# Held conversions, a reciprocal on GpSimd's queue and one store for each chunk of w_out, in a fused attention and soft-MoE kernel

## The chip, the cores and the metric

The kernel runs on one core of a Trainium2 chip. The metric is device time in microseconds of one execution, the median over repeated runs, each measured from outside the kernel. A profile is one further execution, recorded by the hardware profiler; it has its own time and its own span (from the first to the last instruction). TensorE is called PE, VectorE DVE, ScalarE ACT, GpSimd POOL and SyncE SP, as in the profile.

## The reference, cut to what matters

Three layers follow each other. `phi` is the feature map of a linear attention, the second layer has a PReLU with one slope for each hidden column, the third is a soft mixture of experts.

```python
def phi(x):                                        # q, k: 8 x 8 x 576 x 64
    proj = np.einsum('bhsd,df->bhsf', x, w_phi)    # 128 features
    proj = proj - np.max(np.abs(proj), axis=-1, keepdims=True)
    return np.concatenate([np.exp(proj), np.exp(-proj)], axis=-1)
kv  = np.einsum('bhsf,bhsd->bhfd', phi(k), v)
num = np.einsum('bhsf,bhfd->bhsd', phi(q), kv)
den = np.einsum('bhsf,bhf->bhs', phi(q), phi(k).sum(2))[..., None] + 1e-06
x   = (num / den)            # -> 4608 tokens x 512
h   = x @ w_in                                     # 512 x 2048, float64
g   = np.maximum(h, 0.0) + alpha * np.minimum(h, 0.0)
y   = g @ w_out                                    # 2048 x 512, float64
logits = y @ phi_moe                               # 32 slots
d = softmax(logits, over the tokens);  c = softmax(logits, over the slots)
slot_input = d.T @ y;  slot_out[e] = relu(slot_input[e] @ w1[e]) @ w2[e]
out = c @ slot_out
```

[...]

## The kernel before

The 4608 tokens are cut into 12 blocks of 384 and the 2048 hidden columns into 16 chunks of 128. A *slot* is one block times one chunk: 12 matmuls into the tile `ph` (`gemm`, L531 to L541, the instruction is recorded at L538), which multiply x, split into a high and a low part (`xhi`, `xlo`), by a chunk of `w_in`, split likewise. The first slot of a block uses `xhi` in its first eight matmuls and `xlo` in its last four. After a slot, ACT and DVE form the PReLU in `gT` (L545, L546). `ph` has two banks, so a slot can't start before the `gT` of the slot two earlier has been read out of its bank.

Ahead of a block stands the attention of its tokens: `q_pair` makes features of q and from them `num` and `den`; `q_finish` (L461 on) forms the reciprocal of `den` (L466, L467), spreads it over 128 partitions and multiplies `num` by it, and `scale` splits the product into `xhi` (ACT, L484) and `xlo` (DVE, L485). The spreading is done in two ways. For block 0, PE does it by matmuls into `wide` (`spread`, L488). For every other block the reciprocal goes to memory and comes back as a broadcast: two stores `rc_d<-rd` (L470), two loads `bc<-rc_d` (L475), each pair issued by SP, and the multiplication `num<-bc` (L502) waits for them. The features of K (`features`, L283: a maximum at L285, a difference at L287, two exponentials on ACT) feed the matmuls `pkv`, from which `kv` and `zt` are copied (L369, L370), one pair of heads after another; block 0 needs the first four pairs.

`conv` (L185) makes one conversion of one chunk, or of two chunks at a time: two loads into `raw`, `m = Abs` on ACT (L200), then six DVE instructions (L201, L205, L206, L207, L208, and the sum L212). The tile `m` has two buffers, `raw` three. A finished chunk of `w_in` is split into a high part (ACT, L226) and a low part (DVE, L227). A finished chunk of `w_out` is stored to `wo32` by four stores of 32 partitions each (L235), transposed on PE (L240), and multiplied by the slots' matrix (L247, L253, copy L254). A later `m` in the same buffer waits until the stores and the transposes of the earlier one have read it.

The order on each engine is made by the scheduler of the language, which goes through the work by priority and by its own estimates of times; the kernel gives every step a slot number (`at(slot, phase, ...)`, the calls from L685 on) and adds edges of order without a semaphore (`add_manual_dep(..., nosync)`) where one instruction is to stand behind another on its engine. Before, the conversions of chunks 0 to 2 of `w_in` carry such an edge to the features of K (`behind` 2, 3, 3), the others none. All DMAs are issued by SP, in the order of its queue; POOL does the maximum over partitions for the features of q (`mb<-pj`, L423) and some memsets.

Of the kernel before, what the change touches and what calls it, by code (L numbers as in the profile page):

```python
# [11 lines left out]
I32 = mybir.dt.int32  # L12
U32 = mybir.dt.uint32
AF = mybir.ActivationFunctionType
ALU = mybir.AluOpType
AX = mybir.AxisListType
# [45 lines left out]
def attention_prelu_softmoe(ctx: ExitStack, tc, qT, kT, v, wphi, w_in, w_out, alpha, phi, w1, w2, out):  # L62
    nc = tc.nc
# [8 lines left out]
    wo32 = dram.tile([NC, 128, DM], F32, name="wo32")  # L72
    gT_d = dram.tile([NDEF, NC, 128, BT], F32, name="gT_d")
    rc_d = [dram.tile([2, 32, 2, HB], F32, name=f"rc_d{i}") for i in range(2)]
# [13 lines left out]
    nosync = mybir.DependencyInfo(mybir.DependencyClass.NoSync, mybir.DependencyReason.DATA)  # L88
# [94 lines left out]
    done_k = {}  # L183

    def conv(slot, srcs, uses, behind=None):  # L185
        st = {}
        n = len(srcs)

        def load():
            st["raw"] = prep.tile([128, 2, 1024], I32, tag="raw", name="raw", bufs=3)[:, 0:n]  # L190
            for j in range(n):
                nc.sync.dma_start(st["raw"][:, j], srcs[j])

        def first():
            pair = st["raw"].rearrange("p c (n t) -> p c n t", t=2)
            st["low"], high = pair[:, :, :, 0].bitcast(U32), pair[:, :, :, 1]
            m = st["m"] = prep.tile([128, 2, 512], F32, tag="m", name="m", bufs=2)[:, 0:n]
            rest = st["rest"] = high.bitcast(F32)
            mu, ru = m.bitcast(U32), rest.bitcast(U32)
            heads = [nc.scalar.activation(m, high.bitcast(F32), AF.Abs)]  # L200
            heads.append(nc.vector.tensor_scalar(out=m, in0=m, scalar1=F64_LEAST, scalar2=F64_MOST, op0=ALU.max, op1=ALU.min))  # L201
            if behind is not None:
                for ins, other in zip(heads, done_k[behind]):
                    tc.add_manual_dep(ins.ins, other.name, nosync, reason="behind the features of K")
            nc.vector.tensor_scalar(out=mu, in0=mu, scalar1=3, scalar2=0x3FFFFFFF, op0=ALU.logical_shift_left, op1=ALU.bitwise_and)  # L205
            nc.vector.scalar_tensor_tensor(out=mu, in0=high.bitcast(U32), scalar=0xC0000000, in1=mu, op0=ALU.bitwise_and, op1=ALU.bitwise_or)  # L206
            nc.vector.tensor_scalar(out=ru, in0=mu, scalar1=0xFF800000, scalar2=None, op0=ALU.bitwise_and)  # L207
            nc.vector.scalar_tensor_tensor(out=rest, in0=st["low"], scalar=2.0 ** -52, in1=rest, op0=ALU.mult, op1=ALU.mult)  # L208

        def second():  # L210
            m = st["m"]
            mark[slot + 1] = nc.vector.tensor_tensor(out=m, in0=m, in1=st["rest"], op=ALU.add).ins  # L212
            for j, use in enumerate(uses):
                use(slot + j, m[:, j])

        at(slot - 2, "pre", load)
        at(slot, "pre", first)
        at(slot + 1, "pre", second)
# [12 lines left out]
    def use_w_out(c):  # L231
        def use(slot, w):
            st = {}
            for i in range(4):
                nc.sync.dma_start(wo32[4 * i + c // 4, 32 * (c % 4):32 * (c % 4) + 32, :], w[32 * i:32 * i + 32])  # L235

            def trans():
                pt = bank("pwt")
                for k in range(KD):
                    nc.tensor.transpose(pt[:, 128 * k:128 * k + 128], w[:, 128 * k:128 * k + 128], ident)  # L240
                st["wT"] = prep.tile([128, 512], F32, tag="wT", name="wT")
                nc.scalar.copy(st["wT"], pt)

            def product():
                pw = bank("pw", ps_l)
                for k in range(KD):
                    nc.tensor.matmul(pw[32 * k:32 * k + 32, 0:128], phi_sb[:, k, :], st["wT"][:, 128 * k:128 * k + 128], start=True, stop=True)  # L247
                st["sw"] = prep.tile([128, 128], F32, tag="sw", name="sw")
                nc.scalar.copy(st["sw"], pw[:, 0:128])

            def gather():
                pw = bank("pw2", ps_l)
                nc.tensor.matmul(pw[:, 0:32], st["sw"], tident[:, 0:32], start=True, stop=True)  # L253
                nc.vector.tensor_copy(wpr[:, c, :], pw[:, 0:32])  # L254

            at(slot + 2, "pe", trans)
            at(slot + 3, "pe", product)
            at(slot + 4, "pe", gather)
        return use
# [3 lines left out]
    def k_pair(slot, i):  # L263
        b, p = divmod(i, NP)
# [17 lines left out]

        def features(src, dst, nt, read):  # L283
            mx = att.tile([128, 4], F32, tag="mx", name="mx", bufs=4)
            nc.vector.tensor_reduce(out=mx[:, 0:nt], in_=src, axis=AX.X, op=ALU.max, apply_absolute_value=True)  # L285
            neg = dst[:, :, 1, :]
            ins = nc.vector.tensor_tensor(out=neg, in0=src, in1=mx[:, 0:nt].unsqueeze(2).to_broadcast([128, nt, F]), op=ALU.subtract).ins  # L287
            if read is not None:
                read.append(ins)
            nc.scalar.activation(dst[:, :, 0, :], neg, AF.Exp)  # L290
            done_k[i] = nc.scalar.activation(neg, neg, AF.Exp, scale=-1.0).ins, ins
# [95 lines left out]
    xhi_t, xlo_t, q_st = {}, {}, {}  # L387
# [73 lines left out]
    def q_finish(slot, n):  # L461
        st = q_st[n]

        def recip():
            rd = sm.tile([128, BT], F32, tag="dT", name="rd")[:, 0:HB]
            nc.vector.tensor_scalar(out=rd, in0=st["den"][:, 0:HB], scalar1=1e-6, scalar2=None, op0=ALU.add)  # L466
            nc.vector.reciprocal(out=rd, in_=rd)  # L467
            st["rd"] = rd
            for j in range(2 if n else 0):
                nc.sync.dma_start(rc_d[n % 2][j].rearrange("p h t -> h p t"), rd[64 * j:64 * j + 64])  # L470

        def widen():
            bc = st["bc"] = xp.tile([128, NP, BT], F32, tag="bc", name="bc")
            for j in range(2):
                nc.sync.dma_start(  # L475
                    bc[64 * j:64 * j + 64], rc_d[n % 2][j, 0:NP].rearrange("p h t -> p (h t)").unsqueeze(0).to_broadcast([64, NP, BT]))

        def scale(p):
            def go():
                if p == 0:  # L480
                    xhi_t[n] = xp.tile([128, KD, BT], F32R, tag="xhi", name="xhi")
                    xlo_t[n] = xp.tile([128, KD, BT], F32R, tag="xlo", name="xlo")
                xs = st["num"][:, p, :]
                nc.scalar.copy(xhi_t[n][:, p, :], xs)  # L484
                nc.vector.tensor_tensor(out=xlo_t[n][:, p, :], in0=xs, in1=xhi_t[n][:, p, :], op=ALU.subtract)  # L485
            return go

        def spread(p):  # L488
            wide = bank("wide", ps_h)
            together([  # L490
                lambda j=j, h=h, sl=slice(64 * j, 64 * j + 64): nc.tensor.matmul(
                    wide[sl, HB * h:HB * h + HB], ident[sl, 64 * j + 32 * h + p:64 * j + 32 * h + p + 1].to_broadcast([64, 64]), st["rd"][sl],
                    start=True, stop=True)
                for h in range(2) for j in (1, 0)])
            nc.vector.tensor_tensor(out=st["num"][:, p, :], in0=wide[:, 0:BT], in1=st["num"][:, p, :], op=ALU.mult)

        def divide(p):
            def go():
                if n == 0:
                    return spread(p)  # L500
                xs = st["num"][:, p, :]
                ins = nc.vector.tensor_tensor(out=xs, in0=st["bc"][:, p, :], in1=xs, op=ALU.mult).ins  # L502
                tc.add_manual_dep(ins, mark[max(k for k in mark if k <= slot + wait)].name, nosync, reason="behind the load")
            return go

        wait = (1, 3)[n] if n < 2 else 6
        at(slot, "post", recip)
        if n:
            at(slot + 1, "pre", widen)
        for p in range(NP):  # L510
            at(slot + wait, "post", divide(p))
        for p in range(NP):
            at(slot + wait, "post", scale(p))
# [175 lines left out]
    for n in range(NB):  # L689
# [3 lines left out]
            else:  # L693
                q_pair(NC * (n - 1) + 3 * p - 6 - (p > 0) if n > 2 else 12 + 2 * p if n > 1 else (0, 2, 5, 8)[p], n, p)
        q_finish((-22, 12)[n] if n < 2 else NC * (n - 1) + 7, n)
    for c, slot, behind in ((0, -30, 2), (1, -26, 3), (2, -22, 3), (3, -3, None)):
        conv(slot, [w_in[c].bitcast(I32)], [use_w_in], behind)
    for c in range(4, NC, 2):
        conv(c - 4, [w_in[d].bitcast(I32) for d in (c, c + 1)], [use_w_in] * 2)
    for c in range(0, NC, 2):  # L700
        conv(int(10 + 1.2 * c), [w_out[d].bitcast(I32) for d in (c, c + 1)], [use_w_out(d) for d in (c, c + 1)])
    for n in range(NDEF, NB):
# [66 lines left out]
    for step in range(-45, nslots + 4):  # L769
        slot = real.get(step)  # L770
        for fn in sched.get((step, "pre"), ()):
            fn()
        h = None
# [215 lines left out]
```

## Time and profile before

| | |
|---|---|
| runs | median 977.13 us of 3 (976.02 to 977.84) |
| the profiled execution | 975.91 us |
| its span | 973.9 us, mean granted PE clock 0.987 |
| busy: PE, DVE, ACT, POOL | 931.4 (96%), 709.7 (73%), 410.3 (42%), 148.4 (15%) us |
| chain that ended last | PE 79%, DVE 13%, ACT 4%, DMA 2% |

The profiled execution is 2.0 us longer than its span, and 1.2 us shorter than the median. The table says that PE is the bound on average. An average over 974 us hides where PE is not: the trace has to be cut into stretches for that. The granted clock is a factor on PE's speed (1.00 is 2.4 GHz, 0.50 is 1.2 GHz). In rows of the timeline the first number is the start in us from the start of the span, the second the time of the group in us, then engine, line, operation, output<-inputs by tile names, and in brackets the idle time of the engine just before and what ended it.

### The profile page before, as it was taken

What the parts mean: (1) busy time and instruction counts of PE and PEld (TensorE: products, weight loads), DVE (VectorE), ACT (ScalarE), POOL (GpSimd) and SP (SyncE); (2) the same over time, 40 slices, a digit from 0 to 9 for tenths busy, and PEclk for the clock granted to TensorE, in tenths of its full rate; (3) what the DMA queues carried; (4) which work ended last, traced back from release to release, by engine and by line L of the source; (5) the groups of instructions that cost most, each with busy time, mean ns of one, the idle gap of its engine ahead of it and who ended that gap; (6) DMA issues with size and microseconds to landing.
All of it is one profiled execution on the core that took longest, in us unless ns stands there. A gap on an engine that the chain in (4) does not pass through costs nothing.

```text
span 973.9 us, 19896 instructions
## 1 busy us (share of the span) xinstructions
PE 931.4 (96%) x8210; PEld 653.7 (67%) x8210; DVE 709.7 (73%) x1341; ACT 410.3 (42%) x789; POOL 148.4 (15%) x84
## 2 busy tenths in 40 slices
PE   7978996999999999999999999999999999899997
PEld 4546774677767676676677676776777767787444
DVE  6899996897577587767777677777766767865233
ACT  6655654545445334345345336354343351221113
POOL 5111220301201212122021122111021220000000
PEclk9979998999999999999999999999999999999999
DMA  7346665553131131021121121210111508588999
GB/s 262 116 162 206 204 207 154 176 173 114 54 87 34 31 84 44 23 78 44 35 71 42 33 72 31 70 31 23 46 34 51 178 29 269 172 270 265 329 351 327
DMA packets 75382, 121.34 MB, mean 125 GB/s; under 512 B 7836, under 2 KB 49308, under 8 KB 75292
## 3 DMA queue, kind: packets, MB, share of 16 engines
q1 hardware_dynamic: 75292, 120.07, 39.5%
q8 instruction: 65, 1.06, 0.5%
q14 instruction: 25, 0.20, 0.1%
HBM read 99.03 MB, written 21.00 MB: 123 GB/s over the span
## 4 chain that ended last, share of the span: by engine, by line
PE 79%; DVE 13%; ACT 4%; DMA 2%; issue 1%; SPq 0%; ACTq 0%; DVEq 0%
PE ph L538 39%; PE num L444 6%; PE pkv L340 5%; PE pS L643 4%; PE pl L574 4%; PE den L449 3%; PE pq L411 3%; PE pk L297 2%; PE pso L887 2%; PE pe L867 1%; PE po L923 1%; DVE m L206 1%; DVE m L212 1%; PE pt L362 1%; DVE raw L208 1%
## 5 line engine op out<-in xcount | busy, mean ns | idle before, releaser
L538 PE MATMUL ph<-xhi,w 128*128 128x384 f32 x1536 | 433.4, 351 | 11.5 <-ACT xhi L484 6.1
L538 PEld LDWEIGHTS ph<-xhi,w 128*128 128x128 f32 x1536 | 279.4, 189 | 74.6 <-issue 41.0
L538 PE MATMUL ph<-xlo,w 128*128 128x384 f32 x768 | 257.3, 341 | 0.1
L423 POOL PARTITION_ALL_REDUCE mb<-pj x48 | 141.9, 2957 | 468.4 <-ACT pj L417 374.2
L545 ACT ACTIVATE gT<-ph 128x384 f32<-128x384 f32 x192 | 93.7, 489 | 252.6 <-PE ph L538 248.5
L546 DVE SCALAR_TENSOR_TENSOR gT<-gT,alpha_rest,ph 128x384 f32<-128x384 f32 x192 | 115.7, 603 | 109.2 <-ACT gT L545 108.4
L538 PEld LDWEIGHTS ph<-xlo,w 128*128 128x128 f32 x768 | 144.3, 189 | 11.4 <-issue 8.0
L565 DVE STREAM_TRANSPOSE gb<-gT 128x384 f32<-128x384 f32 x162 | 91.8, 571 | 3.0 <-issue 0.2
L433 ACT ACTIVATE qe<-pj 128x768 f32<-128x768 f32 x90 | 71.8, 838 | 26.7 <-DVE pj L427 18.3
L444 PE MATMUL num<-qe,kv 128*64 128x192 f32 (+1 forms) x488 | 70.0, 412 | 3.6 <-ACT kall L290 2.3
L340 PE MATMUL pkv<-kall 128*64 128x256 f32 x464 | 57.5, 391 | 2.9 <-ACT num L454 1.8
L285 DVE TENSOR_REDUCE mx<-pk 128x4 f32<-128x512 f32 (+1 forms) x80 | 49.5, 623 | 10.4 <-PE pk L297 9.1
L290 ACT ACTIVATE kall<-kall 128x512 f32<-128x512 f32 x60 | 37.5, 627 | 37.6 <-DVE kall L287 37.4
L411 PE MATMUL pq<-qraw,wp 64*128 64x384 f32 x192 | 46.6, 544 | 6.5 <-DMA qraw<-in_qT_dram 3.8
L444 PEld LDWEIGHTS num<-qe,kv 128*64 128x64 f32 x488 | 31.2, 136 | 27.8 <-issue 17.9
L328 DVE TENSOR_TENSOR ks<-ks,kall 128x256 f32<-128x256 f32 x96 | 47.5, 511 | 0.4
L340 PEld LDWEIGHTS pkv<-kall 128*64 128x64 f32 x464 | 31.2, 138 | 23.9 <-issue 5.8
L427 DVE TENSOR_TENSOR pj<-pj,mb 128x768 f32<-128x768 f32 x48 | 44.7, 932 | 2.4 <-POOL mb L423 2.4
L449 PE MATMUL den<-qe,zt 128*32 128x192 f32 x720 | 42.0, 337 | 1.7 <-ACT qe L433 1.7
L287 DVE TENSOR_TENSOR kall<-pk,mx 128x512 f32<-128x512 f32 x60 | 40.9, 681 | 2.4 <-PE pkv L340 1.7
L454 ACT COPY num<-num 128x384 f32<-128x384 f32 x48 | 22.7, 476 | 44.2 <-PE num L444 42.5
L297 PE MATMUL pk<-wp,kall 64*128 64x128 f32 x512 | 38.9, 290 | 2.3 <-DMA kall<-in_kT_dram 1.3
(204 smaller groups left out, 1104.5 us busy)
## 6 DMA issues: line engine op xcount, KB each, us to landing
w<-in_w_dram SPq DMA_DIRECT2D x46, 256.0 KB
kall<-in_v_dram SPq DMA_DIRECT2D x30, 320.0 KB
qraw<-in_qT_dram SPq DMA_DIRECT2D x48, 192.0 KB
out_dram<-os SPq DMA_DIRECT2D x18, 512.0 KB
bc<-rc_d SPq DMA_DIRECT2D x22, 384.0 KB
raw<-in_w_in_dram SPq DMA_DIRECT2D x16, 512.0 KB
raw<-in_w_out_dram SPq DMA_DIRECT2D x16, 512.0 KB
gT_d<-gT SPq DMA_DIRECT2D x32, 192.0 KB
```

Of the source, the lines that this page charges most:

```text
L285: nc.vector.tensor_reduce(out=mx[:, 0:nt], in_=src, axis=AX.X, op=ALU.max, apply_absolute_value=True)
L297: lambda t=t, j=j, sl=slice(64 * j, 64 * j + 64): nc.tensor.matmul(st["pk"][:, j, F * t:F * t + F], st["kraw"][sl, 128 * t:128 * t + 128], ...
L340: return lambda: nc.tensor.matmul(pkv[64 * j:64 * j + 64, 0:256], st["vt"][:, t, 64 * j:64 * j + 64], part.rearrange("p s f -> p (s f)"), ...
L411: lambda j=j, sl=slice(64 * j, 64 * j + 64): nc.tensor.matmul(pq[j][:, 0:BT], wp[sl, F * j:F * j + F], st["qraw"][sl], start=True, stop=True)
L423: nc.gpsimd.partition_all_reduce(mb, pj, 128, bass_isa.ReduceOp.absmax)
L433: nc.scalar.activation(st["e", s], pj, AF.Exp, scale=(1.0, -1.0)[s])
L444: lambda s=s, j=j: nc.tensor.matmul(num[64 * j:64 * j + 64, o:o + w], kvs[:, s, 64 * j:64 * j + 64], st["e", s][:, j, o:o + w], start=(s = ...
L449: lambda s=s, j=j, h=h, zt=kv_t[NP * ((n * BT + h * HB) // S) + p][1]: nc.tensor.matmul(den[64 * j + 32 * h:64 * j + 32 * h + 32, 0:HB], z ...
L538: gemm_last[0] = nc.tensor.matmul(h, (w_in_hi, w_in_lo)[a][c][:, 128 * k:128 * k + 128], (xhi, xlo)[b][:, k, :], start=(i == 0), stop=(i = ...
L545: nc.scalar.activation(gT, h, AF.Relu, scale=-1.0)
L546: ins = nc.vector.scalar_tensor_tensor(out=gT, in0=gT, scalar=alpha_rest[:, c:c + 1], in1=h, op0=ALU.mult, op1=ALU.add).ins
L565: nc.vector.transpose(out=half_of(n, c // 8)[:, c % 8, :], in_=gT)
```

## The change

It has three parts. First, all conversions from chunk 2 of `w_in` on, and the maximum of the features of K of pairs 4 and 5, get an edge of order behind block 0's x: on ACT behind its last `xhi`, on DVE behind its last `xlo`. Chunks 2 and 3 get other slots (-19 and -16 for -22 and -3). Second, the reciprocal of block 1 is stored and loaded by POOL's DMA queue (`nc.gpsimd`) where SP's queue did it; the other blocks stay on SP. Third, a chunk of `w_out` is stored by one DMA of 128 partitions, whose target has the shape 4 x 32 x 512, where it was four DMAs of 32 x 512.

```diff
     def use_w_out(c):
         def use(slot, w):
             st = {}
-            for i in range(4):
-                nc.sync.dma_start(wo32[4 * i + c // 4, 32 * (c % 4):32 * (c % 4) + 32, :], w[32 * i:32 * i + 32])
+            nc.sync.dma_start(wo32[c // 4::4, 32 * (c % 4):32 * (c % 4) + 32, :], w)
...
-            nc.vector.tensor_reduce(out=mx[:, 0:nt], in_=src, axis=AX.X, op=ALU.max, apply_absolute_value=True)
+            ins = nc.vector.tensor_reduce(out=mx[:, 0:nt], in_=src, axis=AX.X, op=ALU.max, apply_absolute_value=True).ins
+            if 4 <= i < 6:
+                tc.add_manual_dep(ins, done_k["x", 0][1].name, nosync, reason="behind block 0's x")
...
             for j in range(2 if n else 0):
-                nc.sync.dma_start(rc_d[n % 2][j].rearrange("p h t -> h p t"), rd[64 * j:64 * j + 64])
+                (nc.gpsimd if n == 1 else nc.sync).dma_start(rc_d[n % 2][j].rearrange("p h t -> h p t"), rd[64 * j:64 * j + 64])
...
-                nc.sync.dma_start(
+                (nc.gpsimd if n == 1 else nc.sync).dma_start(
                     bc[64 * j:64 * j + 64], rc_d[n % 2][j, 0:NP].rearrange("p h t -> p (h t)").unsqueeze(0).to_broadcast([64, NP, BT]))
...
-                nc.scalar.copy(xhi_t[n][:, p, :], xs)
-                nc.vector.tensor_tensor(out=xlo_t[n][:, p, :], in0=xs, in1=xhi_t[n][:, p, :], op=ALU.subtract)
+                done_k["x", n] = (
+                    nc.scalar.copy(xhi_t[n][:, p, :], xs).ins,
+                    nc.vector.tensor_tensor(out=xlo_t[n][:, p, :], in0=xs, in1=xhi_t[n][:, p, :], op=ALU.subtract).ins)
...
-    for c, slot, behind in ((0, -30, 2), (1, -26, 3), (2, -22, 3), (3, -3, None)):
+    for c, slot, behind in ((0, -30, 2), (1, -26, 3), (2, -19, ("x", 0)), (3, -16, ("x", 0))):
         conv(slot, [w_in[c].bitcast(I32)], [use_w_in], behind)
     for c in range(4, NC, 2):
-        conv(c - 4, [w_in[d].bitcast(I32) for d in (c, c + 1)], [use_w_in] * 2)
+        conv(c - 4, [w_in[d].bitcast(I32) for d in (c, c + 1)], [use_w_in] * 2, ("x", 0))
```

Every line behind the second hunk is one to two higher in the changed kernel than in the one before. What follows are places of the order of instructions, which has no times.

On DVE, around x of block 0, before: the divisor (`rd`), its reciprocal and the products with `wide`, among conversions (`m`, `raw`, `w`) and features of K (`mx`, `kall`, `kp`).

```order
L466 TENSOR_SCALAR rd<-den 128x192
L205 TENSOR_SCALAR m<-m 128x1024
L427 TENSOR_TENSOR pj<-pj,mb 128x768
L285 TENSOR_REDUCE mx<-pk_645 128x2
L285 TENSOR_REDUCE mx<-pk 128x4
L467 RECIPROCAL rd<-rd 128x192
L227 TENSOR_TENSOR w_617<-m,w_617 128x512
L206 SCALAR_TENSOR_TENSOR m<-raw,m 128x1024
L287 TENSOR_TENSOR kp<-pk_645,mx 128x2x128
L287 TENSOR_TENSOR kall<-pk,mx 128x4x128
L285 TENSOR_REDUCE mx<-pk 128x4
L495 TENSOR_TENSOR num<-wide,num 128x384
```

The same place now, from the last copies of `kv` and `zt` on which block 0 depends to the first instruction behind its x.

```order
L370 COPY kv<-pt 128x256
L371 COPY zt<-pt 128x4
L467 TENSOR_SCALAR rd<-den 128x192
L468 RECIPROCAL rd<-rd 128x192
L497 TENSOR_TENSOR num<-wide,num 128x384
L487 TENSOR_TENSOR xlo<-num,xhi 128x384
L497 TENSOR_TENSOR num<-wide,num 128x384
L487 TENSOR_TENSOR xlo<-num,xhi 128x384
L497 TENSOR_TENSOR num<-wide,num 128x384 x2
L487 TENSOR_TENSOR xlo<-num,xhi 128x384 x2
L284 TENSOR_REDUCE mx<-pk 128x4
```

The divisor, the reciprocal, the products and the four `xlo` stand one behind the other; conversions and features that stood among them come after.

On DVE, around the product of block 1 with its broadcast reciprocal (`num_897<-bc`), before, with the buffers' numbers.

```order
L285 TENSOR_REDUCE mx_1503<-pk4_1496 128x2
L326 TENSOR_TENSOR ks_1568<-kall_97 128x256
L207 TENSOR_SCALAR raw_1337<-m_1459 128x1024
L326 TENSOR_TENSOR ks_1568<-kall_97 128x256
L287 TENSOR_TENSOR kp_1502<-pk4_1496,mx_1503 128x2x128
L502 TENSOR_TENSOR num_897<-bc_1387,num_897 128x384
L328 TENSOR_TENSOR ks_1568<-ks_1568,kall_97 128x256
```

The same place now. `m_1219` holds the first two chunks of `w_out`, `m_1324` the next two and `m_1447` the two behind them, in the buffer of `m_1219`; `L212` is the last step of a conversion and releases its stores.

```order
L212 TENSOR_TENSOR m_1219<-m_1219,raw_1131 128x1024
L428 TENSOR_TENSOR pj_1522<-pj_1522,mb_1527 128x768
L207 TENSOR_SCALAR raw_1226<-m_1324 128x1024
L329 TENSOR_TENSOR ks_1550<-ks_1550,kall_97 128x256
L208 SCALAR_TENSOR_TENSOR raw_1226<-raw_1226 128x1024
L212 TENSOR_TENSOR m_1324<-m_1324,raw_1226 128x1024
L253 COPY wpr_106<-pw2_1467 128x32
L201 TENSOR_SCALAR m_1447<-m_1447 128x1024
L504 TENSOR_TENSOR num_897<-bc_1381,num_897 128x384 x4
L205 TENSOR_SCALAR m_1447<-m_1447 128x1024
```

Directly ahead of the product there now stands a step (`L201`) of a conversion whose buffer was that of `m_1219`, whose last step is eight rows up.

On ACT, around `xhi` of block 1, before.

```order
L249 COPY sw_1487<-pw_1482 128x128
L242 COPY wT_1494<-pwt_1489 128x512
L290 ACTIVATE kp_1502<-kp_1502 128x2x128
L484 CAST xhi_1579<-num_897 128x384
L291 ACTIVATE kp_1502<-kp_1502 128x2x128
L200 ACTIVATE m_1682<-raw_1524 128x1024
L484 CAST xhi_1579<-num_897 128x384 x3
```

The same place now.

```order
L241 COPY wT_1370<-pwt_1365 128x512
L248 COPY sw_1414<-pw_1409 128x128
L241 COPY wT_1421<-pwt_1416 128x512
L200 ACTIVATE m_1447<-raw_1331 128x1024
L486 CAST xhi_1561<-num_897 128x384 x2
L248 COPY sw_1475<-pw_1470 128x128
```

The first step of the conversion `m_1447` stands directly ahead of `xhi`; before, the first step of a conversion stood behind the first `xhi`.

On SP's queue around the reciprocal of block 1, before.

```order
L549 DMA gT_d<-gT 128x384
L235 DMA wo_72<-m 32x512 x8
L549 DMA gT_d<-gT 128x384
L192 DMA raw<-in_w_out_dram 128x1024 x2
L470 DMA rc_d_75<-rd 2x32x192 x2
L273 DMA kall<-in_kT_dram 128x512
L475 DMA bc<-rc_d_75 64x1536 x2
```

On POOL's queue now.

```order
L424 ISA mb<-pj 128x768
L471 DMA rc_d_75<-rd 2x32x192 x2
L476 DMA bc<-rc_d_75 64x1536 x2
L424 ISA mb<-pj 128x768
L365 MEMSET zt 128x128
L424 ISA mb<-pj 128x768
```

The stores and the loads of block 1's reciprocal have left SP's queue, where eight stores of `wo` and other DMAs stood ahead of them, and stand on POOL's between two maxima over partitions.

## Rows read from the trace of the kernel before

**Rows 1.** Windows: stretch; length, busy us by engine (x instructions), PE clock, DMA share, GB/s.

```profile
150.00:175.00 25.00, 18.75 (x129) 13.85 (x131) 20.08 (x35) 12.97 (x26) 3.03 (x2) 0.86 0.52 154
51.30:61.50 10.20, 7.82 (x64) 4.33 (x60) 10.20 (x18) 6.25 (x10) 0.00 (x0) 0.50 0.40 144
...
153.70:160.50 6.80, 5.51 (x22) 3.49 (x23) 6.67 (x14) 3.39 (x8) 0.00 (x0) 0.50 0.20 62
250.00:800.00 550.00, 549.94 (x4601) 387.31 (x4600) 396.15 (x765) 238.24 (x451) 96.03 (x49) 1.00 0.19 53
```

**Rows 2.** Timeline, PE: from block 0's last `den` to slot 2.

```profile
47.66 0.51 PE L449 MATMUL den<-kall,zt 128*32 128x192 f32 x8
...
55.96 2.83 PE L491 MATMUL wide<-rd,ident 64*64 64x192 f32 x16 [2.30 <-DVE rd L467]
...
66.55 0.97 PE L538 MATMUL ph<-xhi,w 128*128 128x384 f32 x4
...
79.50 0.44 PE L538 MATMUL ph<-xhi,w 128*128 128x384 f32 x1 [2.06 <-DVE gT L546]
```

**Rows 3.** Timeline, DVE: x of block 0.

```profile
44.96 0.42 DVE L369 COPY kv<-pt 128x256 f32<-128x256 f32 x1
...
51.90 0.35 DVE L466 TENSOR_SCALAR rd<-den 128x192 f32<-128x192 f32 x1
...
71.04 0.55 DVE L485 TENSOR_TENSOR xlo<-num,xhi 128x384 fp32r<-128x384 f32 x1
```

**Rows 4.** Timeline, DVE: reciprocal and first product of block 1.

```profile
135.78 1.35 DVE L467 RECIPROCAL rd<-rd 128x192 f32<-128x192 f32 x1
...
153.83 0.56 DVE L502 TENSOR_TENSOR num<-bc,num 128x384 f32<-128x384 f32 x1 [6.90 <-DMA bc<-rc_d]
```

**Rows 5.** Timeline, SP's queue: stores of `wo`, block 1's reciprocal.

```profile
134.98 5.23 SPq L235 DMA_DIRECT2D wo<-m  x8
...
141.76 1.19 SPq L470 DMA_DIRECT2D rc_d<-rd  x2
...
147.04 1.47 SPq L475 DMA_DIRECT2D bc<-rc_d  x2
```

**Rows 6.** Timeline, PE: around the first matmul of block 1.

```profile
136.81 0.66 PE L240 MATMUL pwt<-ident,m 128*128 128x128 f32 x4
...
146.99 1.95 PE L340 MATMUL pkv<-kall 128*64 128x256 f32 x16 [1.08 <-DVE kp L287]
154.99 1.33 PE L538 MATMUL ph<-xhi,w 128*128 128x384 f32 x3 [6.05 <-ACT xhi L484]
```

**Rows 7.** Timeline, ACT: one `xhi` of block 0.

```profile
59.90 0.49 ACT L484 CAST xhi<-num 128x384 fp32r<-128x384 f32 x1
```

**Rows 8.** Timeline, POOL: a maximum over partitions while DVE is busy.

```profile
69.91 5.86 POOL L423 PARTITION_ALL_REDUCE mb<-pj  x1 [22.27 <-DVE raw L208]
```

**Rows 9.** Windows: only reciprocal stores of block 2 run; then `wo` stores.

```profile
203.00:203.60 0.60, 0.60 (x6) 0.24 (x6) 0.60 (x3) 0.00 (x0) 0.00 (x0) 1.00 0.13 45
...
208.00:210.00 2.00, 2.00 (x24) 1.07 (x20) 2.00 (x5) 1.10 (x2) 0.00 (x0) 1.00 0.82 237
```

**Rows 10.** Groups by shape: xcount | busy us, mean ns | idle before.

```profile
L328 DVE TENSOR_TENSOR ks<-ks,kall 128x256 f32<-128x256 f32 x96 | 47.5, 511 | 0.4
...
L427 DVE TENSOR_TENSOR pj<-pj,mb 128x768 f32<-128x768 f32 x48 | 44.7, 932 | 2.4 <-POOL mb L423 2.4
...
L212 DVE TENSOR_TENSOR m<-m,raw 128x1024 f32<-128x1024 f32 x14 | 18.2, 1304 | 0.0
...
L208 DVE SCALAR_TENSOR_TENSOR raw<-raw 128x1024 f32<-128x1024 uint32 x14 | 17.0, 1215 | 0.0
...
L200 ACT ACTIVATE m<-raw 128x1024 f32<-128x1024 f32 x14 | 16.2, 1156 | 11.7 <-DVE w L227 9.7 <-DMA wo<-m 1.1 <-PE pwt L240 0.9
...
L207 DVE TENSOR_SCALAR raw<-m 128x1024 uint32<-128x1024 uint32 x14 | 14.7, 1051 | 0.1
...
L201 DVE TENSOR_SCALAR m<-m 128x1024 f32<-128x1024 f32 x14 | 12.9, 919 | 4.1 <-ACT m L200 4.0
```

## The prediction

> **What bounds the kernel now.** I read the windows first, then the timeline of the engines around the two places where the change puts something, then the groups of instructions. The windows show two kinds of stretches [rows 1]. From 250 to 800 us PE is busy 549.94 of 550 us at full clock: nothing that the change does can speed that up, and a microsecond that PE has lost by 250 us comes out at the end, unless the last stage absorbs it. Ahead of that PE has gaps and half clock: in 150 to 175 us it is busy only 18.75 of 25 us, and it runs at 1.2 GHz from 51.3 to 61.5 and from 153.7 to 160.5 us. In the first of these DVE is busy all the time (10.20 of 10.20). So the front of the kernel is DVE's, and the question is what DVE does first, and where it stands still.
>
> Two places matter. x of block 0: the last `den` is through PE at 48.17, `rd` starts at 51.90 because DVE has conversions in between, the reciprocal's matmuls `wide` start at 55.96, and the last `xlo` ends at 71.59; slot 0 starts at 66.55, and slot 2 at 79.50, after a wait for a `gT` that stands behind conversions [rows 2, 3]. x of block 1: its reciprocal ends at 137.13, but the first product runs at 153.83, after DVE has stood still for 6.90 us for `bc` [rows 4]. That is SP's doing: eight stores of `wo` fill its queue from 134.98 to 140.21, the reciprocal's stores are issued at 141.76, its loads at 147.04 [rows 5]. PE waits 6.05 us for the first `xhi` of block 1 and starts slot 16 at 154.99 [rows 6].
>
> **Part 1, conversions behind x of block 0.** The steps from the copy of `kv` are now a chain without filling: `kv` ends at 45.38, `den` at 48.17; `rd` 0.35 and the reciprocal 1.35 bring it to 49.9; two groups of `wide`, 2.83 each at half clock or half of that at full clock, to 52.7 or 55.6; the last product 0.55 (a form like `xlo`), `xhi` 0.49 and `xlo` 0.55 to 54.3 or 57.2 [rows 2 to 4, 7]. The copy itself comes somewhat earlier, since conversions ahead of it go behind too; I take 53. x of block 0 is thus about 18 us earlier. That is not a gain of 18 us: slots 0 and 1 move, slot 2 needs chunk 2, whose conversion now starts behind x, and all the steps that DVE puts off it still has to do before block 1. What counts is DVE's idle time. In the chain of 8.9 us (11.8 at half clock) DVE has 0.35 + 1.35 + 8 x 0.55 = 6.1 us of its own work, so 2.8 to 5.7 us are idle where before it stood still for nothing there. I take 5.5, near the upper end, since PE has little to do then and was at half clock in just this stretch before [rows 1]. The full price is visible only because DVE is the limit; were it not, it would be nothing.
>
> **Part 2, block 1's reciprocal on POOL.** The 6.90 us of DVE's wait go, if POOL's way is ready in time. By the order, DVE's work ahead of the first product, each instruction at its group's mean, is 0.7 us less than before. Without the wait the product would have run at 153.83 - 6.90 = 146.93; with 5.5 us of part 1 and 0.7 less work DVE comes to it at 151.7. The stores and loads cost, on SP, 1.19 us of issue, 4.09 us until the loads are issued, 1.47 us of issue and 5.32 us until DVE goes on: 12.1 us [rows 4, 5]. No row shows them on POOL. Below, they take the same 12.1 us from a reciprocal at 137.1: 149.2. Above, the maximum over partitions that stands ahead in POOL's queue is stretched to 5.86 us, as one was beside a busy DVE [rows 8]: 155.1. I take 151, the middle lowered a little since the reciprocal itself stands earlier in DVE's order now; it is hidden behind what follows. SP loses four issues, which is worth nothing: SP isn't waited for elsewhere there.
>
> **Part 3, one store for each chunk of w_out.** Eight issues of 0.65 us become two (5.23 us to 1.3) [rows 5]. But the data may come out later. While only the two reciprocal stores run, whose target's outer size is 2, the DMA share is 0.13 at 45 GB/s, which is 2 of 16 engines; with the `wo` stores of 32 partitions it is 0.82 at 237 GB/s [rows 9]. The new store's target is 4 x 32 x 512. If its outer size counts likewise, four engines carry it, at about 90 GB/s, and the two stores of a conversion, 512 KB, take 5.8 us; on sixteen they take 2.2. These are the two bounds.
>
> The Trainium skill, "DMA: Bandwidth & Descriptors", in the paragraph on how many engines, says that the engines of a DMA are the largest number up to 16 that divides the outer dimension of both sides. The 0.13 agrees with it for the reciprocal's stores; for the new stores (4 and 128) it gives four engines and so the longer of the two times, where the number of partitions alone would give the shorter. It speaks against this part of the change.
>
> Who waits for that store? The ACT step `m_1447` takes the buffer of `m_1219`, and the change puts it and its DVE step `L201` directly ahead of the product of block 1. Between the end of `m_1219` and the product DVE has `pj` 0.93, `L207` 1.05, `L208` 1.22, `L212` 1.30, `L201` 0.92 and two small steps of some 0.7 together: 6.1 us [rows 10]. So `m_1219` ends at 151.7 - 6.1 = 145.6. Behind it come issue 1.3, data 5.8, the fixed part of a store, 4.09 less 2.2 of data (98 KB at 45 GB/s) = 1.9, `Abs` on ACT 1.16 and `L201` 0.92: 11.1 us, so the product is at 156.7 [rows 4, 5, 9, 10]. With sixteen engines it is 7.5 us and 153.1. I take four engines: the row of the reciprocal stores is nearest in kind.
>
> **The sum.** From the product to slot 16 it was 154.99 - 153.83 = 1.16 us; slot 16 then starts at 157.9, 2.9 us later than before. By the order PE also has less to do ahead of it: one `pkv` group of 1.95 and one group of transposes of 0.66, 2.6 us, stand behind it now [rows 6]. So 5.5 us more have been lost by slot 16. Some comes back: those 2.6 us fill gaps later, some `gT` of block 1 stand about 5 us earlier in DVE's order, and the half clock of 153.7 to 160.5 us, worth up to 3.4 us, may shorten [rows 1]. I bound this by 0 and 3.4 and take 2.5. Sum: +3.0 us, 975.91 + 3.0 = 978.9 for a profiled execution. That one was 1.2 us below the median of the runs, so 980.1: 980.
>
> **The rivals.**
> - *Block 1 starts earlier* (the other side). The store is not what is waited for last (more than four engines, or transposes and issue go faster), the chain of x of block 0 runs at full clock with 2.8 us idle, and the 6.90 us are won nearly whole. The product is then at 146.9 + 2.8 - 0.7 = 149.0, slot 16 at 150.2, 4.8 us earlier, less 2.6 of work put off, plus up to 3.4 of clock regained: about -5, 972. It decides from where the product of block 1 runs before 151. For it: DVE's wait is the longest single one of the front. Against it: the buffer's wait stands right there in the order.
> - *Nothing moves.* Stores on sixteen engines, DVE's idle time only changes its place (5.5 against 6.9): product 153.1, slot 16 0.7 us earlier, 2.6 us put off, 2.5 back: -0.6, 976.5. For it: the same work on the same limiting engine.
> - *POOL is slower than SP.* Its maxima stretch, its issues take longer than SP's, and the broadcast lands after the store's round: beyond 156.7. At 12.1 us doubled from a reciprocal at 137.1 the product is at 161.3, 4.6 us behind the forecast's: 985. Against it: POOL has 148 us of work in the whole span.
> - *The change doesn't do what it says.* The orders show that it does for the first two parts; for the third the engines of a store are in no order. That is the second rival.
>
> **How the numbers follow.** Forecast 0.42 (977 to 985 by itself), nothing moves 0.22, earlier 0.24, POOL slower 0.12. A change of 0.2%, 2.0 us, is about what a measurement of this kernel tells from none. Faster by more: 0.9 x 0.24 + 0.25 x 0.22 + 0.06 x 0.42 = 0.30; within: 0.26; slower: 0.44. The range reaches from the earlier start (971.5) to POOL's delay (986.5).
>
> **What would show it.** Right: the last `xlo` of block 0 ends at 51 to 57; DVE idle 3 to 6 us ahead of it; DVE waits ahead of `L201` of `m_1447` for ACT, and ACT for the store; a DMA share near 0.25 while two `wo` stores run alone; the product of block 1 at 155 to 159, with no wait for `bc`. Wrong: a wait for `bc` on DVE of more than 1 us (POOL), a share near 1 during these stores (sixteen engines), or slot 16 before 152. A loss in the last stage, behind 850 us, or loads of q and K that come late behind slower stores would be something that I have not priced.

## The result and the profile after

The changed kernel takes 989.66 us (median of 4 runs, 988.66 to 994.5), the kernel before 976.58 in the same comparison. The ratio is 1.0144, 95% interval 1.0108 to 1.018: the change costs 13 us. The forecast was 980, slower; the direction came out, the size is more than four times the one forecast. The profiled execution took 989.64 us with a span of 987.5 us, 13.6 us longer than before.

x of block 0 did what the prediction says. (A conversion, below, puts the numbers of a chunk of weights together from pairs of 32-bit integers.) On DVE, after (the columns are as before; where a row has brackets, the engine stood still ahead of it):

```profile
42.15 0.42 DVE L370 COPY kv<-pt 128x256 f32<-128x256 f32 x1 [0.75 <-PE pt L363]
...
45.70 0.36 DVE L467 TENSOR_SCALAR rd<-den 128x192 f32<-128x192 f32 x1 [3.05 <-PE den L450]
...
48.41 0.56 DVE L497 TENSOR_TENSOR num<-wide,num 128x384 f32<-128x384 f32 x1 [0.97 <-PE wide L493]
49.55 0.56 DVE L487 TENSOR_TENSOR xlo<-num,xhi 128x384 fp32r<-128x384 f32 x1 [0.58 <-ACT xhi L486]
...
51.15 0.56 DVE L487 TENSOR_TENSOR xlo<-num,xhi 128x384 fp32r<-128x384 f32 x1 [0.58 <-ACT xhi L486]
...
52.76 1.03 DVE L487 TENSOR_TENSOR xlo<-num,xhi 128x384 fp32r<-128x384 f32 x2
```

The last `xlo` ends at 53.79 (53 forecast; 71.59 before [rows 3]). From 42 us on DVE stands still for 0.75 + 3.05 + 0.97 + 2 x 0.58 = 5.9 us (5.5 forecast). Slot 0 starts at 52.32 instead of 66.55 [rows 2].

The loss is at block 1 and behind it. On DVE, around the product of block 1, and later steps `L201` that wait for ACT too:

```profile
144.44 1.21 DVE L212 TENSOR_TENSOR m<-m,raw 128x1024 f32<-128x1024 f32 x1
...
159.21 0.69 DVE L201 TENSOR_SCALAR m<-m 128x1024 f32<-128x1024 f32 x1 [9.25 <-ACT m L200]
159.82 1.96 DVE L504 TENSOR_TENSOR num<-bc,num 128x384 f32<-128x384 f32 x4
...
186.37 0.69 DVE L201 TENSOR_SCALAR m<-m 128x1024 f32<-128x1024 f32 x1 [6.40 <-ACT m L200]
...
209.40 0.69 DVE L201 TENSOR_SCALAR m<-m 128x1024 f32<-128x1024 f32 x1 [3.55 <-ACT m L200]
```

The wait for `bc` of 6.90 us [rows 4] is gone, and 9.25 us for a conversion stand in its place, directly ahead of the product. `m_1219` ends at 145.65 (145.6 forecast). What ACT waited for (twice for a store, the third time for a load):

```profile
158.05 1.12 ACT L200 ACTIVATE m<-raw 128x1024 f32<-128x1024 f32 x1 [8.97 <-DMA wo<-m]
...
165.62 1.18 ACT L200 ACTIVATE m<-raw 128x1024 f32<-128x1024 f32 x1 [2.76 <-DMA wo<-m]
...
185.22 1.12 ACT L200 ACTIVATE m<-raw 128x1024 f32<-128x1024 f32 x1 [4.17 <-DMA raw<-in_w_out_dram]
```

SP's queue at the same time (start, time of issue):

```profile
145.68 1.26 SPq L234 DMA_DIRECT2D wo<-m  x2
146.99 1.52 SPq L192 DMA_DIRECT2D raw<-in_w_out_dram  x2
149.88 2.46 SPq L234 DMA_DIRECT2D wo<-m  x2
152.38 5.33 SPq L192 DMA_DIRECT2D raw<-in_w_out_dram  x2
```

The two stores of `m_1219` are issued by 146.94, and ACT goes on at 158.05: 11.1 us, where the sum had 7.7. The issues behind them stretch too, from 1.52 to 5.33 us for two loads. PE, and the windows (length, busy us by engine, clock, DMA share, GB/s):

```profile
160.96 1.33 PE L540 MATMUL ph<-xhi,w 128*128 128x384 f32 x3 [8.50 <-ACT xhi L486]
```

```profile
143.60:168.00 24.40, 12.78 (x59) 10.74 (x59) 15.11 (x27) 7.27 (x14) 1.00 (x2) 0.52 0.58 172
147.00:148.00 1.00, 1.00 (x12) 0.47 (x10) 1.00 (x3) 0.44 (x1) 0.23 (x1) 0.50 0.30 39
148.00:149.00 1.00, 0.61 (x10) 0.36 (x2) 0.97 (x2) 0.68 (x2) 0.00 (x0) 0.50 0.19 23
156.00:157.00 1.00, 0.00 (x0) 0.00 (x0) 0.00 (x0) 0.00 (x0) 0.00 (x0) 0.50 0.29 113
250.00:800.00 550.00, 549.94 (x4614) 388.43 (x4612) 399.21 (x774) 236.25 (x450) 98.85 (x50) 1.00 0.20 56
```

A quarter of the sixteen DMA engines is a share of 0.25. The share is near that just after the stores' issue (0.30 and 0.19, at 39 and 23 GB/s) and again just before ACT goes on (0.29, at 113 GB/s). Loads of `raw` and of `bc` are under way in this stretch too, so the rate of the stores alone can't be read here; a run below shows it better. PE's clock is 0.52 over 24.4 us, where before it was 0.50 over 6.8 [rows 1]. From 250 to 800 us nothing has changed: 549.94 of 550 us busy again. The `gT` of the slots, before and after (the last two times are the starts of the first and of the last):

```profile
L545 ACT ACTIVATE gT<-ph x192: 463/491/520, 73.8 to 888.5; 128x384 f32<-128x384 f32 x192
```

```profile
L547 ACT ACTIVATE gT<-ph x192: 468/490/522, 56.9 to 900.2; 128x384 f32<-128x384 f32 x192
```

The last slot is 11.7 us later, and 11.3 of this are there at the 65th (398.21 against 386.91): most of the 13.6 us is lost in the front. The other 1.9 us are in the stage behind the last slot; nothing here explains them.

### The profile page after: what moved, and what is told of

The parts are those of the page before. It is cut to its first block, busy times and chain, and to the rows that moved or that the text cites. A ratio compares the mean times of both kernels' runs of the same rounds, so it can differ in the third digit from the quotient of the medians.

```text
span 987.5 us, 19841 instructions
## 1 busy us (share of the span) xinstructions
PE 934.4 (95%) x8210; PEld 656.3 (66%) x8210; DVE 706.8 (72%) x1341; ACT 409.1 (41%) x789; POOL 152.0 (15%) x88
## 3 DMA queue, kind: packets, MB, share of 16 engines
q8 instruction: 65, 1.06, 0.5%
## 4 chain that ended last, share of the span: by engine, by line
PE 80%; DVE 11%; DMA 3%; ACT 3%; issue 2%; SPq 1%; DVEq 0%; ACTq 0%
PE ph L540 38%; PE num L445 7%; PE pkv L341 6%; PE pS L645 4%; PE pl L576 4%; PE den L450 3%; PE pq L412 3%; PE pk L298 3%; PE pso L889 2%; PE pe L869 1%; PE po L925 1%; PE pt L363 1%; DVE m L206 1%; DMA wo<-m 1%; DVE gT L548 1%
## 5 line engine op out<-in xcount | busy, mean ns | idle before, releaser
L298 PEld LDWEIGHTS pk<-wp,kall 64*128 64x128 f32 x512 | 33.1, 196 | 13.2 <-issue 6.5
```

Of the source, the lines that this page charges most:

```text
L298: lambda t=t, j=j, sl=slice(64 * j, 64 * j + 64): nc.tensor.matmul(st["pk"][:, j, F * t:F * t + F], st["kraw"][sl, 128 * t:128 * t + 128], ...
```

## The experiments

Each part of the change was undone or done alone. Ratios are to the kernel before, with the 95% interval; "hold" is the first part, "POOL" the second, "store" the third.

| hold | POOL | store | median us | ratio |
|---|---|---|---|---|
| - | - | - | 975.62 to 976.96 | 1 |
| yes | - | - | 974.86 | 0.9977 (0.996 to 0.9994) |
| - | yes | - | 976.71 | 0.9999 (0.9989 to 1.001) |
| yes | yes | - | 976.37 | 0.9999 (0.9983 to 1.0016) |
| - | - | yes | 980.03 | 1.0052 (1.0032 to 1.0072) |
| - | yes | yes | 982.32 | 1.0064 (1.0042 to 1.0087) |
| yes | - | yes | 983.22 | 1.008 (1.0053 to 1.0106) |
| yes | yes | yes | 989.66 | 1.0144 (1.0108 to 1.018) |
| yes | yes | 16 engines | 979.48 | 1.0026 (1.0007 to 1.0045) |
| yes | - | 16 engines | 973.89 | 0.9968 (0.995 to 0.9985) |
| conversions only | - | - | 973.46 | 0.9966 (0.9951 to 0.9982) |

Every row without the single store lies at or below the time before, every row with it on four engines above.

**The third part undone.**

```diff
-            nc.sync.dma_start(wo32[c // 4::4, 32 * (c % 4):32 * (c % 4) + 32, :], w)
+            for i in range(4):
+                nc.sync.dma_start(wo32[4 * i + c // 4, 32 * (c % 4):32 * (c % 4) + 32, :], w[32 * i:32 * i + 32])
```

> The changed kernel with its third part undone: a chunk of w_out goes to memory by four stores of 32 partitions again; the held conversions and POOL's queue stay. Theory A (the single store is carried by four DMA engines, lands late, and the conversion of the buffer behind it stands ahead of block 1's product): ACT's wait for the store, 9.0 us in the changed kernel, falls under 2 us, slot 16 starts at 152 to 155 us instead of 161.0, and the time falls to 974 to 980. Theory B (holding the conversions costs the time, by DVE's idle time in the chain of block 0's x and by less PE work ahead of block 1): it stays at 985 to 990.

Measured 976.37 us. Theory A holds for the time, and slot 16 is at 155.39, just outside its bound. ACT still waits 3.37 us for a store, more than the 2 expected, but only 2.0 us after the last of eight issues:

```profile
147.03 4.80 SPq L235 DMA_DIRECT2D wo<-m  x8
```

```profile
153.80 1.14 ACT L200 ACTIVATE m<-raw 128x1024 f32<-128x1024 f32 x1 [3.37 <-DMA wo<-m]
```

The order changes too: `L201` of `m_1447` now stands behind the product, so this run alone doesn't single out the store.

**The store alone.** The edit is the same line the other way round, on the kernel before.

> The kernel before with only the third part of the change: one store for each chunk of w_out. Theory A: the stores land late here too, ACT waits for them ahead of several conversions of w_out, in sum 5 us or more, and the time rises to 980 to 988. Theory B, and theory A's weaker form by which a late store hurts only in the order that the held conversions make: no such wait on the path, 974 to 979.

Measured 980.03 us: the bottom of theory A's range, but by another way than theory A names. No ACT step waits for a store in this trace. Block 1's reciprocal does, and DVE waits for it twice as long as before [rows 4]:

```profile
133.78 1.32 SPq L234 DMA_DIRECT2D wo<-m  x2
...
138.88 3.42 SPq L469 DMA_DIRECT2D rc_d<-rd  x2
...
149.82 1.53 SPq L474 DMA_DIRECT2D bc<-rc_d  x2
```

```profile
156.64 1.96 DVE L501 TENSOR_TENSOR num<-bc,num 128x384 f32<-128x384 f32 x4 [13.95 <-DMA bc<-rc_d]
```

The reciprocal's stores are issued 2.9 us earlier than before (138.88 against 141.76), their issue takes 3.42 instead of 1.19 us, and the loads that wait for them follow 7.5 us later instead of 4.1 [rows 5]. The `wo` stores that stand ahead of them are the nearest cause; that both use the same few engines is argued from the shares, not shown by itself.

**The changed kernel's order with sixteen engines.** This is the cleanest pair: each engine's instructions stand in the same order (but for four of PE's 8210 matmuls, at the very start), and the number of stores and their bytes are the same.

```diff
-            nc.sync.dma_start(wo32[c // 4::4, 32 * (c % 4):32 * (c % 4) + 32, :], w)
+            nc.sync.dma_start(wo32[c], w)
```

> The changed kernel with one difference: the single store of a chunk goes to 128 rows that lie one behind the other, target 128 x 512 instead of 4 x 32 x 512. The rows of w_out thus lie in another order in memory than the later loads take them, so the output isn't the reference's; every engine's order of instructions, the number of stores and their bytes are those of the changed kernel. Theory A: sixteen engines carry the store, it lands 6 us earlier, ACT's first wait for it falls from 9.0 us to 0 to 3, the time is 974 to 981. A rival, that the late landing comes from the broadcast loads and the loads of w_out that run at the same time: the wait stays over 6 us and the time at 985 to 990. Theory B: 985 to 990 too, but with a short wait.

Measured 979.48 us, 10 us less than the changed kernel. SP's issue, ACT's wait and DVE's:

```profile
148.54 1.54 SPq L234 DMA_DIRECT2D wo<-m  x2
```

```profile
154.06 1.13 ACT L200 ACTIVATE m<-raw 128x1024 f32<-128x1024 f32 x1 [2.12 <-DMA wo<-m]
```

```profile
155.23 0.69 DVE L201 TENSOR_SCALAR m<-m 128x1024 f32<-128x1024 f32 x1 [2.41 <-ACT m L200]
...
178.08 0.69 DVE L201 TENSOR_SCALAR m<-m 128x1024 f32<-128x1024 f32 x1 [2.08 <-ACT m L200]
...
201.30 0.69 DVE L201 TENSOR_SCALAR m<-m 128x1024 f32<-128x1024 f32 x1 [3.62 <-ACT m L200]
```

Slot 0 starts 3.1 us later in this trace (55.47 against 52.32), before any `wo` store is issued, so durations are compared here and not places. From the end of the issue (150.08) to ACT it is 4.0 us instead of 11.1, DVE's wait 2.41 instead of 9.25. So the shape of the target is the cause of the 10 us, and both rivals fall. DVE's second wait shrinks as well, from 6.40 to 2.08 us; the third stays (3.55 and 3.62), so it isn't the store's. In the changed kernel's order 0.26% over the kernel before are left.

**The second part undone.**

```diff
-                (nc.gpsimd if n == 1 else nc.sync).dma_start(
+                nc.sync.dma_start(
```

(and likewise for the stores `rc_d`).

> The changed kernel with its second part undone: block 1's reciprocal is stored and loaded by SP's queue again. Theory A: the single store still stands on the path, 985 to 992. The rival that the broadcast loads of POOL's queue slow the store down because they are issued beside it: 978 to 983, with ACT's wait for the store under 5 us.

Measured 983.22 us: between the two ranges. The store takes 8.2 us from the end of its issue (147.57) to ACT:

```profile
146.35 1.22 SPq L234 DMA_DIRECT2D wo<-m  x2
```

```profile
155.80 1.12 ACT L200 ACTIVATE m<-raw 128x1024 f32<-128x1024 f32 x1 [6.04 <-DMA wo<-m]
...
183.72 1.13 ACT L200 ACTIVATE m<-raw 128x1024 f32<-128x1024 f32 x1 [4.63 <-DMA wo<-m]
```

That is near the 7.7 of the prediction, and here the rate of four engines can be read, in the stretch in which ACT's wait ends:

```profile
153.00:157.00 4.00, 0.00 (x0) 0.00 (x0) 0.05 (x1) 1.20 (x2) 0.00 (x0) 0.67 0.25 93
```

The share is 0.25 at 93 GB/s; the prediction had 90. (Whether all these bytes are the store's, the profile doesn't say.) But the loss has another place than in the changed kernel. With the reciprocal on SP, the scheduler puts the product (147.23) ahead of the waiting `L201` (156.95), and slot 16 starts earlier even than before the change (154.99 [rows 6]). PE then stands still in the middle of the slot, for an `xhi` that stands behind ACT's waiting step:

```profile
148.87 1.97 PE L540 MATMUL ph<-xhi,w 128*128 128x384 f32 x5
...
157.37 1.65 PE L540 MATMUL ph<-xhi,w 128*128 128x384 f32 x4 [5.68 <-ACT xhi L486]
```

Why the store takes 11.1 us in the changed kernel and 8.2 here is not separated. There POOL's second load is issued at 146.55, when the stores have just been issued, and the second pair of stores follows at 149.88 instead of 159.84. The Trainium skill, "DMA: Bandwidth & Descriptors", "SWDGE vs HWDGE vs iDMA", says that GpSimd's and the other engines' queues feed different queues inside a DMA engine, which serves them in turn; 8.2 against 11.1 us would fit that, but no run shows it by itself. In time, what POOL costs hardly depends on the store: 6.4 us with four engines (989.66 against 983.22), 5.6 with sixteen (979.48 against the 973.89 below).

**Store and POOL without the hold.** Here the held conversions are undone:

```diff
-    for c, slot, behind in ((0, -30, 2), (1, -26, 3), (2, -19, ("x", 0)), (3, -16, ("x", 0))):
+    for c, slot, behind in ((0, -30, 2), (1, -26, 3), (2, -22, 3), (3, -3, None)):
```

(with the edge on the features and the pairs of chunks taken out too).

> The kernel before with the second and third part of the change, without the held conversions. In the kernel with the single store alone, DVE waited 14.0 us for block 1's broadcast, whose stores stood behind w_out's stores on the same DMA engines. Theory A (the late store hurts through whatever waits for it or stands behind it): off SP's queue the broadcast is no longer behind it, the wait falls to 0 to 5 us, and since without the hold ACT's conversion has slack, the time is 973 to 979. Rival (POOL's queue shares the DMA engines, so the broadcast stays late): a wait of 8 us or more, 979 to 984.

Measured 982.32 us: theory A falls here, and the rival's numbers come out. DVE waits 12.12 us for `bc`, nearly as long as with SP's queue:

```profile
137.00 0.86 POOL L471 DMA_DIRECT2D rc_d<-rd  x1 [1.95 <-DVE rd L468]
144.34 0.70 POOL L471 DMA_DIRECT2D rc_d<-rd  x1 [6.47 <-issue]
```

```profile
156.47 0.56 DVE L504 TENSOR_TENSOR num<-bc,num 128x384 f32<-128x384 f32 x1 [12.12 <-DMA bc<-rc_d]
```

The rival's reason is borne out only in part. The first store of the reciprocal lands 7.0 us after its issue, against 3.8 in the next run, which has POOL's queue without the single store. But from the first issue to the product it is 19.5 us here and 17.5 there: most of the way is POOL's own.

**POOL alone.** The kernel before with the line of the second part.

> The kernel before with only the second part: block 1's reciprocal on POOL's queue. If POOL's way is as fast as SP's quiet one, the wait of 6.9 us for the broadcast falls under 3 us and the time is 970 to 975. If DVE's or PE's other work fills the place, or POOL's stores come as late as SP's did, it is 975 to 979. If POOL is slower: 979 to 984.

Measured 976.71 us, no change, inside the second range. POOL's queue and DVE's wait:

```profile
139.25 0.86 POOL L472 DMA_DIRECT2D rc_d<-rd  x1 [1.94 <-DVE rd L469]
143.37 0.70 POOL L472 DMA_DIRECT2D rc_d<-rd  x1 [3.26 <-issue]
...
144.21 0.56 POOL L477 DMA_DIRECT2D bc<-rc_d  x1
149.62 0.53 POOL L477 DMA_DIRECT2D bc<-rc_d  x1 [4.84 <-DMA rc_d<-rd]
```

```profile
156.76 1.96 DVE L505 TENSOR_TENSOR num<-bc,num 128x384 f32<-128x384 f32 x4 [7.69 <-DMA bc<-rc_d]
```

From the first issue to the product it is 17.5 us; on SP it was 12.1 [rows 4, 5]. POOL begins 2.5 us earlier and arrives 2.9 us later: the second store is issued 3.26 us after the first, and the loads come one at a time. The profile names no wait of the second store, but the first lands 3.8 us after its issue, and the second follows 0.3 us behind that landing. It is so in all five runs with POOL's stores; why is not shown.

**The hold alone.** The first part of the change on the kernel before.

> The kernel before with only the first part: conversions and features held behind block 0's x. By the prediction's sum without store and without POOL: slots 0 and 1 at 52 to 55 us, DVE idle 5 to 6 us ahead of block 0's x, the wait for the broadcast still there but shorter, the time 975 to 980. If the hold alone were worth something (slots 0 to 3 earlier, less half clock): 970 to 975. With the run that has the hold and POOL at 976.4, POOL is worth the difference between the two.

Measured 974.86 us, slightly faster, just inside the second range. The wait for the broadcast, expected shorter, is gone. With the conversions held, SP's queue is no longer full of `wo` stores when the reciprocal comes, and DVE finds `bc` there without a wait:

```profile
138.58 1.19 SPq L472 DMA_DIRECT2D rc_d<-rd  x2
141.59 0.52 SPq L477 DMA_DIRECT2D bc<-rc_d  x1
...
147.00 3.62 SPq L235 DMA_DIRECT2D wo<-m  x8
```

```profile
147.94 1.03 DVE L505 TENSOR_TENSOR num<-bc,num 128x384 f32<-128x384 f32 x2
```

```profile
149.51 1.92 PE L541 MATMUL ph<-xhi,w 128*128 128x384 f32 x5
```

Slot 16 is 5.5 us earlier than before [rows 6]; of this 2 us are left at the end. The hold by itself does what POOL's queue was to do; beside the hold POOL's queue brings nothing (976.37 us, the intervals overlap).

**The hold, SP's queue and sixteen engines.** The edits are those of the two experiments on the target and on POOL, together; rows of w_out lie elsewhere again.

> The hold and the single store with block 1's reciprocal on SP, as in the run that came out 0.8% slower than before, with one difference: the store's target is 128 x 512 rows one behind the other, so rows of w_out lie in another order than the later loads take them and the output isn't the reference's. Order and number of instructions on every engine are those of that run. If four engines are the whole price of the single store, this loses it: ACT's waits for the store (6.0 and 4.6 us) fall under 2 us each and the time to 972 to 977, as with the hold alone. If the order that the scheduler made for the single store is to blame, it stays at 981 to 985.

Measured 973.89 us against 983.22 with four engines. The orders are the same but for one store of `gT` and one load of `raw` that have changed places on SP's queue. At block 1 DVE waits 0.2 us for `bc` and nothing for a conversion; ACT's wait is 0.55:

```profile
147.14 0.80 SPq L234 DMA_DIRECT2D wo<-m  x2
```

```profile
151.09 1.20 ACT L200 ACTIVATE m<-raw 128x1024 f32<-128x1024 f32 x1 [0.55 <-DMA wo<-m]
```

```profile
148.00:149.00 1.00, 1.00 (x6) 0.73 (x4) 0.80 (x2) 0.68 (x2) 0.00 (x0) 0.50 1.06 399
```

The share is 1.06 at 399 GB/s in the window in which the changed kernel had 0.19 at 23 (loads of `raw` run beside the stores in both). In this order merging the stores costs nothing where the target's outer size lets all engines work.

**Only the conversions held.**

```diff
-            if 4 <= i < 6:
+            if False:
```

on the hold alone.

> The hold alone (0.9977 of the time before), but only of the conversions: the features of K of pairs 4 and 5 are free to go ahead of block 0's x. If what the hold costs is DVE's idle time of 5 to 6 us in the chain of block 0's x, the free features fill a part of it (each of their DVE steps is 0.4 to 0.7 us) and the time falls to 971 to 974. If x of block 0 comes later by as much as they take, and nothing else changes, 974 to 977.

Measured 973.46 us, inside the first range: the fastest kernel here, level with the one above, 0.9966 (0.9951 to 0.9982) of the time before. x of block 0 comes later, as the other reading expected (its last `xlo` ends at 58.46 instead of 53.89), and block 1 comes earlier:

```profile
146.53 1.53 PE L541 MATMUL ph<-xhi,w 128*128 128x384 f32 x5 [0.21 <-ACT xhi L487]
```

The interval overlaps that of the whole hold, so that it is better than that is not shown; that it beats the kernel before is.

## Why the prediction was wrong

- **What bounds the kernel: right.** PE is busy from 250 to 800 us in both, and most of the loss is in the front.
- **Part 1: right as far as predicted, but its gain was missed.** x of block 0 (53.79 against 53), DVE's idle time (5.9 against 5.5) and the end of `m_1219` (145.65 against 145.6) came out. The sum booked the hold as a loss by DVE's idle time. Alone it gains 0.23%: it moves w_out's conversions, and with them the `wo` stores, behind the reciprocal on SP's queue. The wait that the second part was to remove goes by the first.
- **Part 2: the wait for `bc` went, as forecast, but by luck.** POOL's second load is issued at 146.55 and lands 10.0 us later, at 156.6, where I took 151; it was hidden only because the store kept DVE until 159.21. In the same order with sixteen engines it lands 4.8 us after its issue, so the slow store delays it too. The rival that POOL is slower than SP is right about POOL's way (17.5 against 12.1 us in the run with POOL alone). Beside the hold and the single store POOL's queue costs 5.6 to 6.4 us. Whether by its longer way or by the product's later place in the order is not separated.
- **Part 3: the mechanism right, the size wrong. This is the first step that failed.** The sum has "data 5.8, the fixed part of a store [...] 1.9", 7.7 us from issue to landing; it was 11.1, and product and slot 16 came at 159.82 and 160.96 instead of 156.7 and 157.9. The rate that I scaled up from two engines was right: 93 GB/s measured with SP's queue, where the store took 8.2 us. The term took the stores as alone on their engines. POOL's loads, loads of `raw` and a second pair of stores ran beside them; that these made the rest of the 11.1 us is argued, and their shares are not separated.
- **The sum: the term "some comes back" has the wrong sign. This is the second step that failed, and the larger one.** I took +5.5 us by slot 16 and -2.5 behind it. By slot 16 it was 5.97 us of start and the 2.6 us of work put off, 8.6. By the end it was 13.6, so 5.0 more were lost behind slot 16. DVE's second wait is a part of it: 6.40 us, and 2.08 in the same order with sixteen engines. There ACT waits for a load of `raw` that SP issues at 176.66, directly behind two such stores. The third wait is none: it stays with sixteen engines, and the kernel before has one of 4.0 us [rows 10]. And the half clock that I hoped would shorten lasted 24 us: PE was busy 12.78 us at half speed, where before it was 5.51 [rows 1], some 3.6 us more lost. 1.9 us are in the last stage. These overlap and are not a sum. I priced the store only up to the start of slot 16; the run with the reciprocal on SP, where slot 16 starts 6.1 us earlier than before and the kernel is 0.8% slower, shows that this start does not tell the loss.
- **The rivals.** "Nothing moves" with sixteen engines gave 976.5, and that kernel measured 979.48. The range ended at 986.5 because its upper end held POOL's delay alone, and neither POOL's loads beside the store nor what waits for DMAs behind slot 16's start.

What stays open: why so few bytes moved in the two windows just after the stores' issue (39 and 23 GB/s), how much each of the other DMAs adds to the 11.1 us, what POOL's queue costs by its way and what by the order, and the 1.9 us of the last stage.

## What to carry to other kernels

Merging DMAs is not free even where fewer issues are wanted: look at the outer size of the target, at what else runs on the same engines, and at who waits for the landing (the next user of the buffer, and the DMAs issued behind) before counting issues saved. Follow a late landing beyond the first instruction that it delays: here more was lost behind slot 16's start than the forecast gave back, and a part of it is the clock that PE loses while it waits. When a change has several parts, one of them may already do what another was meant for; the parts alone and undone tell that, the whole does not.

## What the runs showed of the hardware

Stores with a target of outer size 4 kept four of sixteen DMA engines busy: a share of 0.25 at 93 GB/s in the quietest stretch. Two of 256 KB let ACT go on 8.2 us after their issue, and 11.1 us where POOL's loads and a second pair of stores ran beside them; the same bytes to a 128-row target took 4.0. A load of POOL's queue beside them landed 10.0 us after its issue, and 4.8 beside stores on sixteen engines. Issues behind the slow stores on SP stretched from 1.52 to 5.33 us for two loads; behind the fast ones they took 0.91 and 1.21. On POOL's queue the second of two stores was issued 0.3 us after the first had landed, in all five runs, with no wait named in the profile, and the way of a reciprocal through memory took 17.5 us where SP's took 12.1.
